# Fused hash-masked attention and MLP: one q load, three pairs' stacks and rotated pair orders in batch 0

## The chip, the cores and the metric

The kernel runs on one core of a Trainium2 chip. The metric is the device time of one execution in microseconds (us); the time of the kernel before is the median of three runs.

## The reference

Attention over 4 batches, 8 heads, 768 positions and 64 dimensions per head. Each query and each key gets a 6-bit bucket from the signs of a projection; a score counts only where query and key share a bucket. The attention output, laid out as 3072 rows of 512, goes through a two-layer MLP with a squared ReLU.

```
q_bits = (q @ proj > 0);  k_bits = (k @ proj > 0)        # 6 bits each
mask   = bucket(q_bits) == bucket(k_bits)
scores = where(mask, q @ k.T / 8, -1e9);  attn = softmax(scores)
x      = (attn @ v) as [3072, 512]
out    = relu(x @ w_in)**2 @ w_out                        # 512 -> 2048 -> 512
```

## The kernel before

**Units, visits and stages.** Heads are handled in pairs (`hp` 0 to 3), queries in three parts of 256 (`PARTS`). One *visit* is one batch, one part and one pair; it holds four *units*, each 128 queries of one head against all 768 keys (`unit`, line 811): score matmuls into PSUM (`pS` or `side`), a row maximum on DVE (`line`), the exponential on ACT (`e`), division by the row sum, and a transpose into `aT` (on PE through `pT` in the first four visits, by a DMA transpose of `hl` later). `av` (line 859) multiplies with the values. After the four pairs of a part, `moe` (line 915) runs one MLP stage: `pm` (first layer), `g` (squared ReLU), `po` (second layer), `acc`, `out`. There are 12 parts, so 48 visits, 192 units and 12 MLP stages. Early visits also carry the conversion of the MLP weights into fp16 pieces (`split`, line 626: tiles `room`, `sq`, `win`, `wo`, and four `norm` steps through the PSUM tile `side`).

**Preparation.** Before a pair can be visited, `prep` (line 716) builds its stacks. In batch 0 (`plain`) the stacks are float32: per head one tile with k on partitions 0 to 63 and code rows on 64 to 127, and one with q scaled by 1/8 below and code rows above. The chain is: load k and q of each head (128x768, tile `A` for the even head, `Q` for the odd); `pd`, eight matmul records against the projection `pj` (written into `side`); `bits`, the signs, on ACT; four matmuls `pc` with the sign table `sgn`, each 128x384, also into `side`; each is evicted whole by DVE into `L` (even head) or `M` (odd head), 128x384. Then the lower half of `L` or `M` is moved to the upper half of `A` or `Q`, and a second copy of q, loaded separately into a tile `R` (64x768), is scaled into the lower half of `L` or `M`:

```
move(R[U], M[T], 1.0, HALVES if r0 > 0 else (act, dve))   # A <- L, Q <- M
move(M[T], Rqs[odd], SC)                                  # L <- R, M <- R
out.append(((M, R),))
```

The tags `A`, `Q`, `L`, `M` have two buffers each (line 45), so the stacks of two pairs are on chip at a time. `visits` (line 973) goes through the pairs of batch 0 as 0,1,2,3 then 3,2,1,0 then 0,1,2,3; `ready` (line 977) prepares a pair again when its tiles have been given away. That makes eight preparations in batch 0: four in part 0, pairs 1 and 0 in part 1, pairs 2 and 3 in part 2. Pair 1 of part 1 takes the buffers of pair 2, which is visited directly before it. Batches 1 to 3 use fp16 stacks and another branch of `prep`.

**What sets the order.** The kernel records all operations and then orders them itself (class `Program`, line 132). `forward` (line 388) is a list scheduler over the five queues PE, DVE, ACT, POOL and SP with a price for each operation (`cost`, line 200), and picks the engine where an operation may run on several (`move` with ACT, DVE, POOL). `backward` (line 344) gives new priorities from the end, `replay` (line 302) prices the order; `order` (line 253) repeats this `ROUNDS` = 4 times and keeps the cheapest. The queues are in order, so each instruction waits behind the one ahead of it on its engine. `emit` (line 471) puts throwaway matmuls (`idle`) where the planner sees PE idle early on. SP issues nearly all DMAs; ACT issues the loads of `cst`, `pj` and half of the sign table (`acc<-consts`) at the start. `pr.first` makes SP's other loads come after the first pair's loads in the planner's order.

Of the kernel before, what the change touches and what calls it, by code (L numbers as in the profile page):

```python
# [14 lines left out]
F32 = mybir.dt.float32  # L15
# [4 lines left out]
ALU = mybir.AluOpType  # L20
# [22 lines left out]

ALIGN_ON = ("pool",)
BUFS = dict(xx=16, hl=3, e=3, aT=3, g=2, A=2, Q=2, L=2, M=2, RV=2, VV=6)
PRICE = dict(pe=1, dve=3.57, act=0.3, pool=3.06, sp=0.43)
# [3 lines left out]

ROUNDS, BEHIND = 4, 40000
TRIALS, WIDTH, SEED = 0, 3000.0, 1
LOADS = 0

MV = ("act", "dve", "pool", "sp")

# [11 lines left out]
FIRST = len(WIN_AT)  # L68

PACE = ((8, 0), (30, 60), (193, 800))  # L70

# [8 lines left out]
SWITCH, ENTRY = 95, 105  # L80
TRANSPOSES = 165

# [46 lines left out]
class Program:  # L129
# [39 lines left out]
    def add(self, *ways):  # L169
# [12 lines left out]
        for rec, w, (p0, p1, f0, f1, fs, g0, g1) in used:  # L182
            if rec.before is not None:
                deps |= rec.before.ops
            for j, w2, (a0, a1, b0, b1, bs, c0, c1) in rec.accesses:
                if (w or w2 or rec.kind == "psum") and a0 < p1 and p0 < a1 and b0 < f1 and f0 < b1 and not (fs and fs == bs and (c1 <= g0 or g1 <= c0)):
                    deps.add(j)
        for rec, w, r in used:
            rec.ops.add(i)
            rec.accesses.append((i, w, r))  # L190
        deps.discard(i)
# [8 lines left out]
    def cost(key, name, args, kw):  # L200
# [19 lines left out]
        if name.startswith("dma"):  # L220
            b = int(np.prod(args[0].shape)) * mybir.dt.size(args[0].dtype)
            inside = name == "dma_start_transpose" or kinds[:2] == ["sb", "sb"]
            busy = 1040 if key == "pool" else (650 if inside else 475) + 50 * (key == "act")
            return busy, b / (TRANSPOSES if name == "dma_start_transpose" else 314)
        if key == "act":
# [76 lines left out]
    def replay(self, out):  # L302
# [3 lines left out]
        at, free = dict.fromkeys(keys, 0), dict.fromkeys(keys, 0.0)  # L306
        started, dma, dge, held, kind = set(), 0.0, 0.0, 0.0, None
        for _ in out:
            best = None
            for k in keys:  # L310
                if at[k] < len(queues[k]):
                    i = queues[k][at[k]]
                    o = ops[i]
                    if all(j in started for j in o.deps) and all(j in started for j in o.after):
                        t = max([free[k]] + [ops[j].end + LAG * LAGS.get((ops[j].queue.key, k), 200) for j in o.deps])
                        if best is None or t < best[0]:
                            best = t, k, i
            t, k, i = best
            o = ops[i]
            at[k] += 1  # L320
            started.add(i)
            _, _, _, _, (busy, done), port = next(w for w in o.ways if w[0].key == k)
# [191 lines left out]
def lsh_attention_moe(ctx: ExitStack, tc, kq, v, proj2, w_in, w_out, consts, out):  # L514
# [7 lines left out]

    HALVES = tuple(getattr(pr, k) for k in MV)

# [36 lines left out]

    cst = sb([P, 4], F32, "cst")
    act.dma_start(cst, consts[:, 0:4])
    pj = sb([P, 32], F32, "pj")
    dve.memset(pj, 0.0)
    act.dma_start(pj[:, 0:NB], proj2[:, NB : 2 * NB])
    act.dma_start(pj[:, NB : 2 * NB], proj2[:, 3 * NB : 4 * NB])
    sgn_f = sb([P, RT, DM], F32, "acc")[:, 0]
    dve.memset(sgn_f, 0.0)
    for n in range(4):  # L570
        for t in range(2):
            c0 = 4 + t * D
            (act, sp)[t].dma_start(sgn_f[32 * n + t * NB : 32 * n + (t + 1) * NB, n * P + t * D : n * P + (t + 1) * D], consts[2 * t * NB : (2 * t + 1) * NB, c0 : c0 + D])
    sgn = sb([P, 4 * P], BF16, "sgn")
    dve.tensor_copy(sgn, sgn_f)
    thr = sb([P, 1], F32, "thr")
    dve.memset(thr, -(2.0**-80))
# [138 lines left out]
    def prep(b, hp, plain):  # L716
        r0 = pr.rank
        Rs, Rqs = [], []
        n0 = len(pr.ops)
        for odd in range(2):  # L720
            R = sb([P, S], F32, "Q" if odd else "A") if plain else sb([P, S], F32, "R", 2)
            send(R, kq[b, 2 * hp + odd])
            Rs.append(R)
            if plain:
                Rq = sb([P, S], F32, "R", 2)[T]
                send(Rq, kq[b, 2 * hp + odd, U])
                Rqs.append(Rq)
        if r0 < 0:

            pr.first = list(range(n0, len(pr.ops)))  # L730

# [7 lines left out]
        for odd, R in enumerate(Rs):  # L739
            pr.rank = r0  # L740
            if plain:
                M = sb([P, S], F32, "M" if odd else "L")
            else:

# [12 lines left out]
            for half in range(2):  # L757
                w = slice(half * HS, (half + 1) * HS)
                n = 2 * odd + half
                pc = small("pc")[:, 0:HS]  # L760
                pe.matmul(pc, sgn[:, n * P : (n + 1) * P], bits, start=True, stop=True)
                dve.tensor_scalar(M[:, w], pc, cst[:, 0:1], cst[:, 1:2], ALU.subtract, ALU.max)
            if plain:

                move(R[U], M[T], 1.0, HALVES if r0 > 0 else (act, dve))
                move(M[T], Rqs[odd], SC)
                out.append(((M, R),))
# [8 lines left out]
    def scale_values(b):  # L776

        r0 = pr.rank
        tops = sb([P, H // 2], F32, "vtop", 2)
        for hp in range(H // 2) if b else reversed(range(H // 2)):  # L780
            pr.rank = r0 + LOADS * hp
# [190 lines left out]

    visits = [(b, hp, part) for b in range(B) for part in range(PARTS) for hp in (range(H // 2) if b or part % 2 == 0 else reversed(range(H // 2)))]
    kept, kept_v = {}, {}
# [71 lines left out]
```

## Time and profile before

| | us |
|---|---|
| median of 3 runs (882.6 to 884.94) | 884.44 |
| the profiled execution | 885.79 |
| its span in the trace | 884.0 |
| PE busy in the span | 842.0 |
| DVE busy | 663.8 |
| ACT busy | 660.6 |
| POOL busy | 116.4 |

Times of rows are counted from the start of the span. A matmul row's duration is its latency: matmuls are pipelined, so several records overlap and a busy PE need not be at its peak pace. PEld is the weight load, which overlaps PE. A bracket behind a row gives the engine's idle time before it and what released it. The granted clock is the share of TensorE's full clock in a stretch.

### The profile page before, as it was taken

What the parts mean: (1) busy time and instruction counts of PE and PEld (TensorE: products, weight loads), DVE (VectorE), ACT (ScalarE), POOL (GpSimd) and SP (SyncE); (2) the same over time, 40 slices, a digit from 0 to 9 for tenths busy, and PEclk for the clock granted to TensorE, in tenths of its full rate; (3) what the DMA queues carried; (4) which work ended last, traced back from release to release, by engine and by line L of the source; (5) the groups of instructions that cost most, each with busy time, mean ns of one, the idle gap of its engine ahead of it and who ended that gap; (6) DMA issues with size and microseconds to landing.
All of it is one profiled execution on the core that took longest, in us unless ns stands there. A gap on an engine that the chain in (4) does not pass through costs nothing. (4 is left out here: it accounts for less than half of the span.)

```text
span 884.0 us, 17160 instructions
## 1 busy us (share of the span) xinstructions
PE 842.0 (95%) x6403; PEld 548.8 (62%) x6403; DVE 663.8 (75%) x1447; ACT 660.6 (75%) x1148; POOL 116.4 (13%) x182
## 2 busy tenths in 40 slices
PE   8889888899999899999999999999999999999997
PEld 5456544556555566766656667666656666667664
DVE  4789989987688788887686889885886888871111
ACT  3878857678697788887787989887886888873342
POOL 0464324254010010000000100000001000000000
PEclk9999979999999999999999999999999999999999
DMA  5745979975786688789387888897665877672000
GB/s 156 246 127 154 268 171 240 210 174 102 173 182 167 150 148 160 136 152 185 87 188 171 170 144 160 151 180 159 121 112 137 150 151 141 127 144 60 1 24 24
DMA packets 303731, 130.44 MB, mean 148 GB/s; under 512 B 280480, under 2 KB 288288, under 8 KB 303648
## 3 DMA queue, kind: packets, MB, share of 16 engines
q1 hardware_dynamic: 303168, 129.34, 68.8%
q8 instruction: 50, 0.82, 0.4%
q14 instruction: 33, 0.27, 0.1%
q10 hardware_dynamic: 480, 0.01, 0.0%
HBM read 42.02 MB, written 6.29 MB: 55 GB/s over the span
## 5 line engine op out<-in xcount | busy, mean ns | idle before, releaser
L501 PE MATMUL pm<-xx,win 128*128 128x256 f16 x2304 | 296.5, 273 | 2.9 <-ACT g L501 2.0
L501 PE MATMUL po<-wo,g 128*128 128x512 f16 x1152 | 291.3, 379 | 3.5 <-ACT acc L501 1.4
L501 PEld LDWEIGHTS <-win 128*128 128x128 f16 x2304 | 224.2, 98 | 67.8 <-issue 15.3
L501 DVE SCALAR_TENSOR_TENSOR hl<-e,rv,hl 128x768 f16<-128x768 f32 x176 | 178.4, 1017 | 22.0 <-ACT hl L501 20.6
L501 PEld LDWEIGHTS <-g 128*128 128x128 f16 x1152 | 111.2, 98 | 115.4 <-issue 9.8
L501 ACT ACTIVATE hl<-e,rv 128x768 f16<-128x768 f32 x169 | 156.1, 928 | 10.6 <-DMA aT<-hl 6.2
L501 ACT ACTIVATE g<-g 128x512 f32<-128x512 f32 (+1 forms) x185 | 115.7, 626 | 8.9 <-PE po L501 5.9
L499 DVE TENSOR_REDUCE line<-pS 128x1 f32<-128x768 f32 x113 | 107.4, 951 | 17.5 <-PE pS L501 16.5
L501 POOL TENSOR_SCALAR rv<-sm 128x1 f32<-128x1 f32 x99 | 35.8, 362 | 596.6 <-ACT e L501 591.2
L501 DVE SCALAR_TENSOR_TENSOR g<-g,g 128x512 f16<-128x512 f32 x85 | 59.2, 696 | 68.7 <-ACT g L501 68.2
L501 ACT ACTIVATE g<-pm 128x512 f32<-128x512 f32 x96 | 56.7, 590 | 60.6 <-PE pm L501 56.3
L494 PE MATMUL pA<-aT,VV 128*64 128x256 f16 x1584 | 94.9, 274 | 0.0
L494 PEld LDWEIGHTS <-VV 128*64 128x64 f16 x1584 | 83.1, 110 | 15.4 <-issue 14.5
L501 ACT ACTIVATE e<-pS,pair 128x768 f32<-128x768 f32 x72 | 71.0, 986 | 21.3 <-DVE pair L499 16.1
L501 ACT ACTIVATE e<-side,pair 128x768 f32<-128x768 f32 x72 | 70.9, 985 | 16.9 <-DVE rv L501 8.9
L499 DVE TENSOR_REDUCE line<-side 128x1 f32<-128x768 f32 x79 | 75.1, 951 | 5.3 <-PE side L501 5.0
L501 ACT ACTIVATE e<-pS,line 128x768 f32<-128x768 f32 x41 | 36.7, 895 | 20.4 <-DVE line L499 17.0
L501 PEld LDWEIGHTS <-room 128*128 128x128 f16 x288 | 27.3, 98 | 24.1 <-DMA room<-room 3.1
L501 PE MATMUL pS<-A,L 128*128 128x384 f32 x84 | 34.9, 538 | 5.1 <-ACT e L501 2.2
L501 PE MATMUL pS<-room 128*128 128x384 f16 x144 | 32.6, 329 | 2.5 <-DMA room<-room 2.3
L501 PE MATMUL pS<-Q,M 128*128 128x384 f32 x80 | 30.2, 500 | 3.9 <-ACT e L501 3.3
L501 DVE RECIPROCAL rv<-rv 128x1 f32<-128x1 f32 x192 | 30.2, 159 | 4.2 <-POOL rv L501 0.4
(154 smaller groups left out, 913.6 us busy)
## 6 DMA issues: line engine op xcount, KB each, us to landing
R<-kq SPq DMA_DIRECT2D x24, 384.0 KB
room<-w_in SPq DMA_DIRECT2D x16, 511.8 KB
room<-w_out SPq DMA_DIRECT2D x16, 511.8 KB
V<-vp SPq DMA_DIRECT2D x16, 384.0 KB
out<-acc SPq DMA_DIRECT2D x24, 256.0 KB
room<-room SPq DMA_DIRECT2D x60, 96.0 KB
Q<-kq SPq DMA_DIRECT2D x8, 384.0 KB
A<-kq SPq DMA_DIRECT2D x8, 384.0 KB
```

Source lines behind the costliest of these rows:

```text
L494: ins = q.engine.matmul(*map(real, args), **kw).ins
L499: issue(q, getattr(q.engine, name)(*map(real, args), **{k: real(x) for k, x in kw.items()}).ins)
L501: ins = getattr(q.engine, o.name)(*map(real, o.args), **{k: real(x) for k, x in o.kw.items()}).ins
```

## The change

In `prep`, batch 0's branch no longer loads q a second time. The scaled q is taken from the upper half of `A` or `Q` at once (`L<-A`, `M<-Q`, 64x768), and each `pc` is evicted by halves: the lower half straight into the upper half of `A` or `Q` on DVE (64x384), the upper half into the upper half of `L` or `M` on ACT (a ReLU with the bias `floor`) or on DVE. The first preparation uses both banks of `side` in turn for `pc`. `A`, `Q`, `L`, `M` get three buffers, and batch 0 visits the pairs as 0,1,2,3, then 1,2,3,0, then 2,3,0,1: six preparations, four in part 0, pair 0 in part 1 and pair 1 in part 2. Of the constants, the sign table's second half goes to POOL's queue, `pj` is one DMA, and the planner puts SP's other loads behind all of them. `align`, which rescales `wo` after the first MLP stage, may use ACT beside POOL. The planner searches 24 rounds and assumes a lower load rate (265 in place of 314); the other edits in the planner's code keep its rules and make it faster.

```diff
-ALIGN_ON = ("pool",)
-BUFS = dict(xx=16, hl=3, e=3, aT=3, g=2, A=2, Q=2, L=2, M=2, RV=2, VV=6)
+ALIGN_ON = ("act", "pool")
+BUFS = dict(xx=16, hl=3, e=3, aT=3, g=2, A=3, Q=3, L=3, M=3, RV=2, VV=6)
...
-ROUNDS, BEHIND = 4, 40000
+ROUNDS, BEHIND = 24, 40000
...
+START = ((0, 1, 2, 3), (1, 2, 3, 0), (2, 3, 0, 1))
...
-TRANSPOSES = 165
+TRANSPOSES, HBM = 165, 265
...
-    act.dma_start(pj[:, 0:NB], proj2[:, NB : 2 * NB])
-    act.dma_start(pj[:, NB : 2 * NB], proj2[:, 3 * NB : 4 * NB])
+    act.dma_start(pj[:, 0 : 2 * NB].rearrange("p (a k) -> p a k", a=2), proj2[:, NB : 5 * NB].rearrange("p (a k) -> p a k", a=2)[:, :, 0:NB])
...
-            (act, sp)[t].dma_start(sgn_f[32 * n + t * NB : 32 * n + (t + 1) * NB, n * P + t * D : n * P + (t + 1) * D], consts[2 * t * NB : (2 * t + 1) * NB, c0 : c0 + D])
+            (act, pool)[t].dma_start(sgn_f[32 * n + t * NB : 32 * n + (t + 1) * NB, n * P + t * D : n * P + (t + 1) * D], consts[2 * t * NB : (2 * t + 1) * NB, c0 : c0 + D])
...
+    floor = sb([P, 1], F32, "floor")
+    dve.memset(floor, 1.0 - NB / 2)
...
-            if plain:
-                Rq = sb([P, S], F32, "R", 2)[T]
-                send(Rq, kq[b, 2 * hp + odd, U])
-                Rqs.append(Rq)
...
-            pr.first = list(range(n0, len(pr.ops)))
+            pr.first = list(range(n0, len(pr.ops))) + constants
...
                 M = sb([P, S], F32, "M" if odd else "L")
+                move(M[T], R[U], SC)
...
-                pc = small("pc")[:, 0:HS]
+                pc = side[:, n % 2, 0:HS] if r0 < 0 else small("pc")[:, 0:HS]
                 pe.matmul(pc, sgn[:, n * P : (n + 1) * P], bits, start=True, stop=True)
-                dve.tensor_scalar(M[:, w], pc, cst[:, 0:1], cst[:, 1:2], ALU.subtract, ALU.max)
+                if not plain:
+                    dve.tensor_scalar(M[:, w], pc, cst[:, 0:1], cst[:, 1:2], ALU.subtract, ALU.max)
+                    continue
+                dve.tensor_scalar(R[U, w], pc[T], cst[T, 0:1], cst[T, 1:2], ALU.subtract, ALU.max)
+                pr.add((act, "activation", (M[U, w], pc[U], AF.Relu), {"bias": floor[U]}),
+                       (dve, "tensor_scalar", (M[U, w], pc[U], cst[U, 0:1], cst[U, 1:2], ALU.subtract, ALU.max), {}))
             if plain:
...
-                move(R[U], M[T], 1.0, HALVES if r0 > 0 else (act, dve))
-                move(M[T], Rqs[odd], SC)
                 out.append(((M, R),))
...
-    visits = [(b, hp, part) for b in range(B) for part in range(PARTS) for hp in (range(H // 2) if b or part % 2 == 0 else reversed(range(H // 2)))]
+    visits = [(b, hp, part) for b in range(B) for part in range(PARTS) for hp in (range(H // 2) if b else START[part])]
```

What this does to the order is seen at three places. The first is PE's queue at the first preparation of part 1. The numbers behind the names tell buffers apart: before, `A_1089` and `Q_1182` are the new pair's loads and `pS_1305` the scores of its first unit; after, `A_849` and `Q_983` are the new pair's, and `Q_200`, `A_261`, `Q_298` belong to pairs that are still on chip. Before:

```order
L494 MATMUL side_145<-A_1089,pj_63 32x384 x2
L494 MATMUL side_145<-Q_1182,pj_63 32x384 x2
...
L501 MATMUL pm_1293<-xx_917,win_685 128x256
L501 LDWEIGHTS sgn_161
L501 MATMUL side_145<-bits_1263,sgn_161 128x384
L501 MATMUL pS_1305<-A_1089,L_1281 128x384 x2
```

After, on the same engine:

```order
L501 MATMUL side_163<-A_849,pj_69 32x384 x2
L501 MATMUL side_163<-Q_983,pj_69 32x384 x2
L508 MATMUL pS_1083<-Q_200,M_368 128x384 x2
...
L508 MATMUL pS_1140<-A_261,L_449 128x384 x2
...
L508 MATMUL pS_1218<-A_261,L_449 128x384 x2
...
L508 MATMUL pS_1255<-Q_298,M_484 128x384 x2
...
L508 MATMUL pS_1319<-Q_298,M_484 128x384 x2
...
L508 MATMUL pS_1351<-A_849,L_887 128x384 x2
```

Before, the first scores behind the new pair's `pd` are that pair's own; now the scores of five units of other pairs stand between.

The second is SP's queue at the start, before:

```order
L501 DMA Q<-kq 128x768
L501 DMA A<-kq 128x768
L501 DMA acc<-consts 6x64 x4
L501 DMA R<-kq 64x768 x2
L501 DMA A<-kq 128x768
L501 DMA Q<-kq 128x768
L501 DMA unit_f<-consts 128x128
L501 DMA R<-kq 64x768 x2
```

And after:

```order
L508 DMA Q<-kq 128x768
L508 DMA A<-kq 128x768
L508 DMA unit_f<-consts 128x128
L508 DMA A<-kq 128x768
L508 DMA Q<-kq 128x768
L508 DMA room<-w_in 128x2047 x2
L508 DMA V<-vp 128x768 x4
```

The four small loads of the sign table are gone from SP (POOL has them), the `R` loads are gone, `unit_f` comes third, and weights and values come ahead of the third pair.

The third is DVE's queue from the sign table (`sgn`) to the first row maximum (`line0`), before:

```order
L501 CAST sgn_161<-acc_69 128x512
L501 TENSOR_SCALAR L_195<-side_145,cst_65 128x384 x2
L501 TENSOR_SCALAR A_80<-L_195 64x768
L501 TENSOR_SCALAR M_223<-side_145,cst_65 128x384
L501 CAST ident_238<-unit_f_163 128x128
L501 TENSOR_SCALAR M_223<-side_145,cst_65 128x384
L501 TENSOR_SCALAR Q_67<-M_223 64x768
L501 TENSOR_SCALAR M_223<-R_155 64x768
L499 TENSOR_REDUCE line0_74<-pS_242 128x1
```

And after:

```order
L508 TENSOR_SCALAR M_104<-Q_67 64x768
L508 TENSOR_SCALAR L_109<-A_81 64x768
L508 CAST ident_169<-unit_f_86 128x128
L508 CAST sgn_171<-acc_63 128x512
L508 TENSOR_SCALAR A_81<-side_163,cst_65 64x384 x2
L508 TENSOR_SCALAR M_227<-Q_106 64x768
L508 TENSOR_SCALAR Q_67<-side_163,cst_65 64x384 x2
L506 TENSOR_REDUCE line0_77<-pS_231 128x1
```

The moves of q now stand ahead of the sign table, and five instructions, not eight, stand between it and the first row maximum.

## Rows read from the trace of the kernel before

**Rows 1.** The profile page: busy us of each engine, share of the span, instructions

```profile
PE 842.0 (95%) x6403; PEld 548.8 (62%) x6403; DVE 663.8 (75%) x1447; ACT 660.6 (75%) x1148; POOL 116.4 (13%) x182
```

**Rows 2.** Windows: stretch, length, busy us (instructions) of PE, PEld, DVE, ACT, POOL; clock, DMA

```profile
25.00:100.00 75.00, 68.26 (x406) 41.79 (x405) 65.41 (x138) 60.59 (x117) 36.93 (x51) 1.00 0.63 184
100.00:125.00 25.00, 20.01 (x124) 10.68 (x123) 20.63 (x39) 14.00 (x24) 4.74 (x7) 0.80 0.83 224
125.00:175.00 50.00, 42.99 (x268) 25.87 (x267) 48.34 (x97) 37.44 (x65) 18.59 (x24) 1.00 0.99 218
...
300.00:800.00 500.00, 494.25 (x4033) 330.66 (x4032) 406.26 (x897) 416.45 (x717) 27.38 (x65) 1.00 0.78 150
```

**Rows 3.** Groups of PE in 100 to 125 us: count, busy us, mean ns, idle before

```profile
L501 PE MATMUL pS<-A,L 128*128 128x384 f32 x8 | 5.9, 887 | 1.1 <-ACT L L501 1.1
L494 PE MATMUL side<-A,pj 128*32 128x384 f32 x8 | 2.3, 673 | 0.0
```

**Rows 4.** The same view, 50 to 75 us

```profile
L501 PE MATMUL pS<-A,L 128*128 128x384 f32 x16 | 6.2, 499 | 0.9 <-ACT e L501 0.9
```

**Rows 5.** PE's timeline, 105 to 120 us: start, us, what, [idle before, releaser]

```profile
107.11 0.49 PE L494 MATMUL side<-A,pj 128*32 128x384 f32 x2
...
109.49 0.39 PE L501 MATMUL side<-sq,ones 128*128 128x512 bf16 x1 [0.85 <-DVE towin L501]
...
110.91 0.39 PE L501 MATMUL pm<-xx,win 128*128 128x256 f16 x2 [0.87 <-DVE win L501]
...
112.95 2.93 PE L501 MATMUL pS<-A,L 128*128 128x384 f32 x4 [1.15 <-ACT L L501]
...
117.52 0.61 PE L501 MATMUL side<-sq,ones 128*128 128x512 bf16 x1 [1.32 <-DVE M L501]
118.06 0.85 PE L494 MATMUL side<-A,pj 128*32 128x384 f32 x2
```

**Rows 6.** The chain of waits: start, us, work, count

```profile
598.99 0.78 PE pd L494 x8
...
819.24 2.62 PE pm L501 x24
```

**Rows 7.** Groups over the whole span, by line

```profile
L501 DVE TENSOR_SCALAR L<-side,cst 128x384 f32<-128x384 f32 x12 | 8.0, 668 | 1.7 <-PE side L501 1.7
...
L501 ACT ACTIVATE L<-R 64x768 f32<-64x768 f32 x7 | 5.9, 836 | 5.1 <-DVE A L501 5.1
...
L501 ACT ACTIVATE aT<-pT 128x384 f32<-128x384 f32 x26 | 11.9, 485 | 0.2
...
L501 ACT ACTIVATE bits<-pd,thr 128x384 bf16<-128x384 f32 x14 | 8.1, 576 | 7.2 <-PE pd L494 7.2
```

**Rows 8.** Timeline of the start

```profile
1.68 4.47 SPq L501 DMA_DIRECT2D acc<-consts  x4
2.13 2.50 ACTq L501 DMA_DIRECT2D acc<-consts  x4
...
7.58 0.43 DVE L501 CAST sgn<-acc 128x512 bf16<-128x512 f32 x1 [4.78 <-DMA acc<-consts]
...
8.97 0.33 PE L501 MATMUL side<-bits,sgn 128*128 128x384 bf16 x1
...
11.13 0.56 DVE L501 TENSOR_SCALAR A<-L 64x768 f32<-64x768 f32 x1
...
12.62 2.85 PE L501 MATMUL pS<-A,L 128*128 128x384 f32 x8
14.52 0.23 DVE L501 CAST ident<-unit_f 128x128 bf16<-128x128 f32 x1 [2.12 <-DMA unit_f<-consts]
...
15.96 0.55 DVE L501 TENSOR_SCALAR M<-R 64x768 f32<-64x768 f32 x1
16.43 1.81 DVE L499 TENSOR_REDUCE line<-pS 128x1 f32<-128x768 f32 x2
```

**Rows 9.** DMA issues: tile, queue, count, KB each

```profile
R<-kq SPq DMA_DIRECT2D x16, 192.0 KB
```

More of the change, by code (lines that the diff above doesn't have):

```diff
@@ L49 @@
 AHEAD, DELAY, LAG = 60, 2500, 1.0
-ROUNDS, BEHIND = 4, 40000
+ROUNDS, BEHIND = 24, 40000
 TRIALS, WIDTH, SEED = 0, 3000.0, 1
 LOADS = 0
-MV = ("act", "dve", "pool", "sp")
 PREP, STACKS, VALUES = -9, 0, 2
@@ L183, in add @@
             if rec.before is not None:
-                deps |= rec.before.ops
+                deps |= {j for j, _, _ in rec.before.accesses}
             for j, w2, (a0, a1, b0, b1, bs, c0, c1) in rec.accesses:
@@ L189, in add @@
             rec.ops.add(i)
+            if (w or rec.kind == "psum") and not r[4]:
+                rec.accesses = [x for x in rec.accesses if x[0] == i or not (r[0] <= x[2][0] and x[2][1] <= r[1] and r[2] <= x[2][2] and x[2][3] <= r[3])]
             rec.accesses.append((i, w, r))
@@ L223, in cost @@
             busy = 1040 if key == "pool" else (650 if inside else 475) + 50 * (key == "act")
-            return busy, b / (TRANSPOSES if name == "dma_start_transpose" else 314)
+            return busy, b / (TRANSPOSES if name == "dma_start_transpose" else HBM)
         if key == "act":
@@ L306, in replay @@
         at, free = dict.fromkeys(keys, 0), dict.fromkeys(keys, 0.0)
-        started, dma, dge, held, kind = set(), 0.0, 0.0, 0.0, None
+        left = [len(o.deps) + len(o.after) for o in ops]
+        gaps = {(a, k): LAG * LAGS.get((a, k), 200) for a in keys for k in keys}
+        dma, dge, held, kind, soon = 0.0, 0.0, 0.0, None, dict.fromkeys(keys)
         for _ in out:
@@ L312, in replay @@
                     i = queues[k][at[k]]
[L313 to L317, printed above, removed]
+                    if not left[i]:
+                        if soon[k] is None:
+                            soon[k] = max([free[k]] + [ops[j].end + gaps[ops[j].queue.key, k] for j in ops[i].deps])
+                        if best is None or soon[k] < best[0]:
+                            best = soon[k], k, i
             t, k, i = best
@@ L320, in replay @@
             at[k] += 1
-            started.add(i)
+            soon[k] = None
+            for j in o.users:
+                left[j] -= 1
             _, _, _, _, (busy, done), port = next(w for w in o.ways if w[0].key == k)
@@ L521, in lsh_attention_moe @@
     T, U = slice(0, D), slice(D, P)
-    HALVES = tuple(getattr(pr, k) for k in MV)
     def send(out, x):
@@ L558, in dr @@
         return pr.tile(drp, "dram", shape, dtype, name, bufs, tag)
-    cst = sb([P, 4], F32, "cst")
-    act.dma_start(cst, consts[:, 0:4])
     pj = sb([P, 32], F32, "pj")
     dve.memset(pj, 0.0)
-    act.dma_start(pj[:, 0:NB], proj2[:, NB : 2 * NB])
-    act.dma_start(pj[:, NB : 2 * NB], proj2[:, 3 * NB : 4 * NB])
+    act.dma_start(pj[:, 0 : 2 * NB].rearrange("p (a k) -> p a k", a=2), proj2[:, NB : 5 * NB].rearrange("p (a k) -> p a k", a=2)[:, :, 0:NB])
     sgn_f = sb([P, RT, DM], F32, "acc")[:, 0]
@@ L572, in lsh_attention_moe @@
             c0 = 4 + t * D
-            (act, sp)[t].dma_start(sgn_f[32 * n + t * NB : 32 * n + (t + 1) * NB, n * P + t * D : n * P + (t + 1) * D], consts[2 * t * NB : (2 * t + 1) * NB, c0 : c0 + D])
+            (act, pool)[t].dma_start(sgn_f[32 * n + t * NB : 32 * n + (t + 1) * NB, n * P + t * D : n * P + (t + 1) * D], consts[2 * t * NB : (2 * t + 1) * NB, c0 : c0 + D])
+    cst = sb([P, 4], F32, "cst")
+    act.dma_start(cst, consts[:, 0:4])
     sgn = sb([P, 4 * P], BF16, "sgn")
     dve.tensor_copy(sgn, sgn_f)
+    constants = [i for i, o in enumerate(pr.ops) if o.ways[0][1] == "dma_start"]
+    floor = sb([P, 1], F32, "floor")
+    dve.memset(floor, 1.0 - NB / 2)
     thr = sb([P, 1], F32, "thr")
@@ L717, in prep @@
         r0 = pr.rank
-        Rs, Rqs = [], []
+        Rs = []
         n0 = len(pr.ops)
@@ L779, in scale_values @@
         tops = sb([P, H // 2], F32, "vtop", 2)
-        for hp in range(H // 2) if b else reversed(range(H // 2)):
+        for hp in range(H // 2) if b else START[1]:
             pr.rank = r0 + LOADS * hp
```

## The prediction

> **What bounds the kernel now.** I read the page first: PE is busy 842.0 of 884.0 us, DVE and ACT three quarters of it [rows 1]. So the kernel is a PE kernel, and the question is where PE is kept from its work. The windows tell this by stage [rows 2]. From 300 to 800 us PE idles 5.75 of 500 us; nothing in batch 0's preparations can be gained there. The loss lies early: PE idles 6.7 us of 75 from 25 to 100 us (2.25 in each 25), 5.0 of 25 from 100 to 125, and 7.0 of 50 from 125 to 175. In the stretch from 100 to 125 us the granted clock is 0.80 on the mean, the only one of these stretches below 1.00. DVE is 87% busy from 25 to 100 us, 83% from 100 to 125 and 97% from 125 to 175. Batch 0 is thus close to DVE's limit as well, and this will be the main rival.
>
> The groups price the clock: the float32 score records took 5.9 us for 8 of them from 100 to 125 us [rows 3], and 6.2 us for 16 from 50 to 75 us [rows 4], so 0.74 against 0.39 us each. PE's timeline shows why PE stood still [rows 5]: the new pair's `pd` at 107.11 us, then every step waits for one eviction or for a step queued ahead of it on DVE (0.85, 0.87, 1.15 and 1.32 us, released by `towin`, `win`, the ACT write of `L`, and `M`), and the scores of that pair come at 112.95 us, 5.8 us after its `pd`, with almost nothing between. Behind the idle stretch the same `pd` takes 0.85 us where it took 0.49: the lower of the two clock levels (1.2 and 2.4 GHz) was granted there.
>
> At the start [rows 8] the first scores begin at 12.62 us, 3.65 us after the first `pc` at 8.97, because the four `pc` are evicted one after another. The first row maximum is at 16.43, since DVE has the moves of 0.56 and 0.55 us to do and also waits 2.12 us for `unit_f`.
>
> **The change, part by part.** All sums stand against the profiled execution, 885.79 us; the median of the three runs is 1.35 us lower.
>
> *Third buffer and rotated orders.* Part 1's first new pair used the buffers of the pair visited just before it, so its chain could not start earlier. Now, by PE's order, the scores of five units of other pairs stand between `pd` and the new pair's first scores, and they fill what PE idled. What can come back from 100 to 125 us is the idle time of 5.0, plus the clock: 8 score records by 0.35 = 2.8, and two `pd` groups by 0.85 - 0.49 = 0.36, so 0.7. That is 8.5; I leave the 2.25 us that the stretch before idles too, so 6.25. From 125 to 175 us PE idles 2.5 us over that same rate; part of this hangs on the second preparation there, and I take half, 1.25. Term: **7.5 us**. Its ends are 0, if DVE sets the pace anyway, and 8.75.
>
> *Two preparations fewer.* Each costs PE one `pd` group of 0.78 us [rows 6] and four `pc` of at most 0.33 [rows 8]. Twice that is 4.2 us; without the `pc`, whose latencies overlap with their neighbours, 1.6. I take **3.0**. PE's work at the end is back to back (24 `pm` in 2.62 us, 109 ns each [rows 6]), so work removed from PE moves the end by its own length.
>
> *Evictions by halves.* Before, eight preparations cost DVE 32 evictions of 0.67 us [rows 7] and seven moves of 0.55 (five `A<-L` or `Q<-M`, two `M<-R`), 25.3 us; ACT had 23 moves of 0.84 us [rows 7], 19.3. By the order after, DVE has 24 lower halves and 7 upper halves and 3 moves; ACT has 17 upper halves and 7 moves. A half has the same 384 columns on 64 partitions. The trace has no such form, so I bound it by the whole eviction, 0.67 us, and by the cheapest 64-partition form, the 768-column move of 0.55 us; I take 0.67, the row with PSUM as its source. On ACT it lies between `aT<-pT` at 0.485 and `bits` at 0.576 [rows 7]; I take 0.5. So DVE has 22.4 us (2.9 less) and ACT 14.4 (4.9 less). On PE's path this is nothing by itself: it runs beside the matmuls. It is the room that DVE gives for the first term.
>
> *The start.* The first two `pc` go to two banks, and a half on DVE runs beside a half on ACT. The first scores need one pair of halves, not two whole evictions, a move of 0.56 and an ACT move of 0.84: about 2 us sooner than 12.62. DVE's moves of q now stand ahead of `sgn`, in time that it idled (4.78 us), and `unit_f` comes third on SP. The first row maximum could come up to 3.6 us sooner. Ends 0 and 3.6; I take **2.5**.
>
> *Constants on POOL's queue.* SP's four small loads took 4.47 us to issue, ACT's four 2.50 [rows 8]. `sgn` began at 7.58 us, released by them. No row shows a load issued by POOL. From below: if it issues as ACT does, `sgn` is no later, and `bits` is the next to be waited for, so nothing is gained. From above: four at SP's 1.12 us each, behind POOL's own start, and as long again to land put `sgn` up to 4 us later. I take 0, nearest to SP's rows, and keep 4 as an end. A page speaks against this part: the Trainium skill, "SBUF — State Buffer", "SBUF: two separate sides", says that a DMA issued from GpSimd waits for its descriptors while VectorE runs an instruction that takes both port pairs. No run here shows it yet. By that rule the two q moves on DVE would hold up POOL's loads, and the sum would be the late-constants rival's instead of mine.
>
> *Loads and queues.* 16 loads of 192 KB vanish [rows 9], and four of 384 KB with the two preparations. Nothing in the chain waits for them in these stretches, so I cost them at nothing; the cover is PE's other work, and DMA is 0.63 to 0.99 busy there [rows 2], so a gain of some tenths is possible. SP now queues 1 MB of weights and 1.5 MB of values ahead of the third pair's loads; what they delay has two visits to spare. Part 1's load of `A` waits in SP's queue until the old pair's visit is over; behind it stand two weight and two value loads and the first transposes, which `av` waits for. I cost that at 0, as the transposes come after that visit too. `align` on two engines, the planner's new rate and 24 rounds: 0, no wait for `wo` is in these rows.
>
> Sum: 7.5 + 3.0 + 2.5 = 13.0. 885.8 - 13.0 = 872.8; at the median's level, less 1.35, **871.5 us**. This can only be had if DVE follows: from 25 to 175 us it idles 15.6 us [rows 2], more than the 7.5 asked of it, and it has 2.9 us less to do.
>
> **The rivals.**
>
> *DVE sets batch 0's pace.* For it: 97% from 125 to 175 us, and in part 1 the waits are released by DVE. Against it: 83% where PE stands still. Then the stall only moves, and the gain is DVE's removed work and the start: 2.9 + 2.5 = 5.4, so 879.0 us.
>
> *Constants late.* For it: POOL's four loads are on the only chain at the start, which has no other work for PE. Against it: `sgn` has until `bits` is done, about 8 us. It loses the start's 2.5 and up to 2 us more: 876.0 us.
>
> *A thinner cover, slower than before.* The whole order is made new, so the 500 us that PE now fills to 98.9% may be filled worse: where MLP matmuls lie further from the waits of a score unit, PE stands behind it in its queue. DVE and ACT at 81 and 83% there [rows 2] speak against it; that these orders have never met this trace speaks for it. It decides the sign once PE idles more than 13 us beyond its 5.75 there, 2.6% of the stretch; at 16 us the time is 887.5 us.
>
> **How the numbers follow.** The forecast has 0.60, with a range of its own from 864 to 878. DVE's pace 0.20, late constants 0.12, the thinner cover 0.08. The range reaches from 863, where the first and third terms come whole (8.75, 4.2 and 3.6 are 16.6, and some tenths for the loads and for a better order), to 883, which takes in both milder rivals. About 0.3% (2.7 us) is what a measurement of this kernel can tell from no change, so faster means below 881.8. The forecast gives 0.59 of that, the first rival 0.16 (it may end 3 us higher), the second 0.11: faster 0.86. Same: 0.07, from the upper ends of all cases. Slower: 0.07, nearly all from the last rival.
>
> **What would show each step.** Right: no stretch of 25 us between 25 and 230 us with PE idle over 3 us or a clock below 0.95; the first scores near 10.6 us and the first row maximum near 13; batch 0's `pd` records down from 64 to 48; ACT halves near 0.5 us. DVE's pace: PE idle is unchanged in sum from 25 to 200 us while DVE is above 95%. Late constants: DVE's cast of `sgn` after 9 us with DMA as its releaser. Thinner cover: PE's idle from 300 to 800 us above 10 us. The forecast is wrong if the span is above 878 us with the stall gone, since then the time went to a wait that these rows do not have.

## The result and the profile after

| | before | after |
|---|---|---|
| median, us (4 runs each, on one chip) | 884.49 (882.6 to 884.94) | 869.96 (868.34 to 871.95) |
| ratio after to before, 95% interval | | 0.9841 [0.9814, 0.9867] |
| the profiled execution, us | 885.79 | 869.22 |
| its span in the trace, us | 884.0 | 867.1 |

The change takes 14.5 us off. The forecast was 871.5. The total agrees; it did not come together as the sum had it.

The profile page of the kernel after, busy us of each engine, answers to [rows 1]. DVE and ACT are as busy as before; PE has 9.1 us less.

```profile
PE 832.9 (96%) x6347; PEld 544.4 (63%) x6349; DVE 661.8 (76%) x1444; ACT 660.6 (76%) x1150; POOL 111.2 (13%) x182
```

The windows after (stretch, length, busy us and instructions of PE, PEld, DVE, ACT, POOL, then clock, DMA share, GB/s) answer to [rows 2]:

```profile
25.00:100.00 75.00, 66.57 (x381) 38.99 (x384) 68.82 (x153) 62.84 (x123) 35.77 (x46) 1.00 0.51 142
100.00:125.00 25.00, 21.83 (x156) 13.39 (x155) 22.70 (x44) 15.61 (x28) 12.39 (x16) 1.00 0.80 187
125.00:175.00 50.00, 44.70 (x278) 27.59 (x276) 45.53 (x100) 33.05 (x58) 13.17 (x16) 0.93 0.84 187
...
230.00:300.00 70.00, 68.46 (x505) 44.03 (x504) 57.77 (x146) 60.36 (x106) 3.87 (x9) 1.00 0.74 166
300.00:800.00 500.00, 497.33 (x4080) 334.33 (x4079) 395.52 (x871) 405.92 (x702) 23.69 (x65) 1.00 0.75 146
```

One window of the kernel before that the forecast had no row of:

```profile
230.00:300.00 70.00, 64.67 (x486) 40.45 (x484) 53.00 (x142) 50.81 (x90) 3.09 (x5) 0.98 0.70 163
```

The stretch from 100 to 125 us has its full clock back, and PE idles 3.17 us there, not 4.99. But from 25 to 100 us PE now idles 8.43 us (6.74 before), and from 125 to 175 us 5.30 (7.01), at a clock of 0.93. Taken together from 25 to 175 us, idle time fell from 18.74 to 16.90 us only. The gain that no term had stands further back: from 230 to 300 us PE idles 1.54 us in place of 5.33, and from 300 to 800 us 2.67 in place of 5.75.

The row maxima on DVE's timeline serve as milestones: there are 192, one to a unit, and the 13th, 25th, 37th, 61st and 192nd are shown (start, us, what, idle before). Before:

```profile
56.85 0.95 DVE L499 TENSOR_REDUCE line<-pS 128x1 f32<-128x768 f32 x1
...
115.92 0.96 DVE L499 TENSOR_REDUCE line<-pS 128x1 f32<-128x768 f32 x1 [1.09 <-PE pS L501]
...
175.25 0.95 DVE L499 TENSOR_REDUCE line<-side 128x1 f32<-128x768 f32 x1
...
309.52 0.96 DVE L499 TENSOR_REDUCE line<-pS 128x1 f32<-128x768 f32 x1 [0.41 <-PE pS L501]
...
788.61 0.95 DVE L499 TENSOR_REDUCE line<-side 128x1 f32<-128x768 f32 x1
```

After:

```profile
55.18 0.96 DVE L506 TENSOR_REDUCE line<-pS 128x1 f32<-128x768 f32 x1 [0.40 <-PE pS L508]
...
101.23 0.96 DVE L506 TENSOR_REDUCE line<-pS 128x1 f32<-128x768 f32 x1 [0.20 <-PE pS L508]
...
171.00 0.96 DVE L506 TENSOR_REDUCE line<-side 128x1 f32<-128x768 f32 x1
...
294.90 0.96 DVE L506 TENSOR_REDUCE line<-pS 128x1 f32<-128x768 f32 x1 [0.52 <-PE pS L508]
...
769.96 0.95 DVE L506 TENSOR_REDUCE line<-side 128x1 f32<-128x768 f32 x1
```

The lead over the kernel before is 1.7 us at the 13th, 14.7 at the 25th (the old stall lies just ahead of it), 4.25 at the 37th, 14.6 at the 61st and 18.65 at the last. A milestone says nothing of the MLP work that was done or put off between, so the lead at one of them is not all kept. At the 25th nearly all of it is work put off: until then PE had been busy for 100.34 us before and for 86.70 us after. The rise to 14.7 and the fall to 4.25 therefore measure no stall; the windows do.

From 150 us PE falls to its lower clock again. PE's timeline, and the windows at the low clock, first the old stall in the kernel before, then this place:

```profile
149.43 0.38 PE L508 MATMUL side<-sq,ones 128*128 128x512 bf16 x1 [1.81 <-ACT sq L508]
151.12 2.93 PE L508 MATMUL pS<-Q,M 128*128 128x384 f32 x4 [1.31 <-ACT e L508]
153.84 4.00 PE L508 MATMUL pm<-xx,win 128*128 128x256 f16 x22
```

```profile
112.17:122.41 10.24, 8.14 (x19) 2.96 (x19) 6.68 (x10) 4.29 (x7) 1.69 (x3) 0.50 0.67 205
```

```profile
149.95:156.78 6.83, 5.66 (x18) 3.44 (x19) 6.37 (x16) 1.62 (x3) 0.77 (x1) 0.50 0.82 243
```

Two waits of 1.81 and 1.31 us lie ahead of four score records that take 2.93 us; at 109.97 us, at full clock, four of the same kind took 1.56. So in this execution the price of the old stall is paid again, in part, 40 us later. It is not paid in each. The second of the four kernels with added DVE work (below) has the same order and nothing added before about 171 us, and it kept its clock behind the same two waits:

```profile
149.02 0.38 PE L513 MATMUL side<-sq,ones 128*128 128x512 bf16 x1 [1.81 <-ACT sq L513]
150.71 1.56 PE L513 MATMUL pS<-Q,M 128*128 128x384 f32 x4 [1.31 <-ACT e L513]
152.10 2.56 PE L513 MATMUL pm<-xx,win 128*128 128x256 f16 x22
```

These records took 2.81 us less there. Of the four executions of the change itself the fastest, 868.34 us, had a mean granted clock of 1.000 and the others 0.995 to 0.998.

### The profile page after: what moved, and what is told of

The parts are those of the page before. It is cut to its first block, busy times and chain, and to the rows that moved or that the text cites. A ratio compares the mean times of both kernels' runs of the same rounds, so it can differ in the third digit from the quotient of the medians.

```text
span 867.1 us, 17038 instructions
## 1 busy us (share of the span) xinstructions
PE 832.9 (96%) x6347; PEld 544.4 (63%) x6349; DVE 661.8 (76%) x1444; ACT 660.6 (76%) x1150; POOL 111.2 (13%) x182
## 3 DMA queue, kind: packets, MB, share of 16 engines
HBM read 37.30 MB, written 6.29 MB: 50 GB/s over the span
## 4 chain that ended last, share of the span: by engine, by line
PE 61%; DVE 3%; ACT 3%; DMA 3%; issue 1%; POOL 0%; SPq 0%; ACTq 0%; DVEq 0%
PE po L508 22%; PE pm L508 21%; PE pA L501 8%; PE side L508 5%; PE pS L508 5%; DMA aT<-hl 2%; DVE hl L508 1%; ACT e L508 1%; PE pd L501 1%; DVE line L506 1%; DMA A<-A 1%; PE pc L508 1%; ACT hl L508 1%; ACT g L508 0%; ACT acc L508 0%
## 5 line engine op out<-in xcount | busy, mean ns | idle before, releaser
L508 ACT ACTIVATE hl<-e,rv 128x768 f16<-128x768 f32 x167 | 153.9, 928 | 6.1 <-DMA aT<-hl 2.5
L506 DVE TENSOR_REDUCE line<-pS 128x1 f32<-128x768 f32 x113 | 107.4, 951 | 14.5 <-PE pS L508 13.8
L508 POOL TENSOR_SCALAR rv<-sm 128x1 f32<-128x1 f32 x97 | 31.9, 329 | 544.4 <-ACT e L508 541.9
L501 PEld LDWEIGHTS <-VV 128*64 128x64 f16 x1584 | 83.2, 110 | 14.7 <-issue 13.2
L508 DVE SCALAR_TENSOR_TENSOR xx<-pA,xx 128x256 f16<-128x256 f32 x44 | 18.4, 418 | 25.8 <-ACT xx L508 25.2
L508 PE MATMUL pS<-A,L 128*128 128x384 f32 x84 | 33.0, 504 | 3.9 <-ACT e L508 3.7
L508 ACT ACTIVATE xx<-pA 128x256 f16<-128x256 f32 x42 | 15.9, 378 | 24.1 <-PE pA L501 23.9
```

The lines of the kernel that those rows point to most:

```text
L501: ins = q.engine.matmul(*map(real, args), **kw).ins
L506: issue(q, getattr(q.engine, name)(*map(real, args), **{k: real(x) for k, x in kw.items()}).ins)
L508: ins = getattr(q.engine, o.name)(*map(real, o.args), **{k: real(x) for k, x in o.kw.items()}).ins
```

## The experiments

Two questions were put. Which part of the change brings the time: the third buffer with the rotated orders, the halves, or the longer search? And does DVE set batch 0's pace? Ratios are to the kernel before on the same chip, with their 95% intervals.

**The change with four rounds.**

```diff
-ROUNDS, BEHIND = 24, 40000
+ROUNDS, BEHIND = 4, 40000
```

> The changed kernel with the order search back at 4 rounds, all else as changed. Buffers theory (the third buffer and the rotated orders carry the gain): 870 to 875 us, and PE idle from 100 to 125 us still near 3 us. Search theory (the longer search carries it): 880 to 885 us. DVE theory (batch 0 runs at DVE's pace and gains what DVE no longer does): 870 to 875 us.

Measured: 884.41 us, 0.9998 [0.9974, 1.0023]. All of the gain is gone, as the search theory had it. But from 100 to 125 us PE idles only 2.87 us, which is the sign that the buffers theory gave:

```profile
100.00:125.00 25.00, 22.13 (x130) 13.55 (x129) 20.84 (x38) 18.98 (x33) 9.47 (x14) 0.93 0.84 184
```

The largest piece of what is lost lies behind it: from 175 to 230 us PE idles 7.76 us, in the change 2.23. The windows of that place, PE's timeline inside them and two rows of ACT's:

```profile
205.00:215.00 10.00, 5.50 (x49) 3.17 (x44) 9.67 (x18) 9.93 (x11) 2.51 (x2) 0.90 0.54 113
215.00:225.00 10.00, 9.99 (x62) 6.61 (x62) 5.91 (x13) 6.29 (x11) 0.19 (x1) 0.75 0.17 33
```

```profile
207.42 0.52 PE L501 MATMUL pd<-A,pj 128*32 128x384 f32 x2 [0.54 <-issue]
...
209.63 0.33 PE L508 MATMUL pc<-bits,sgn 128*128 128x384 bf16 x1
212.35 0.34 PE L508 MATMUL pc<-bits,sgn 128*128 128x384 bf16 x1 [2.39 <-DVE L L508]
...
215.01 0.48 PE L508 MATMUL pc<-bits,sgn 128*128 128x384 bf16 x1 [1.57 <-ACT L L508]
```

```profile
209.06 5.29 ACT L508 ACTIVATE wo<-wo,rel 128x1024 f16<-128x1024 f16 x5
214.38 0.57 ACT L508 ACTIVATE L<-pc,floor 64x384 f32<-64x384 f32 x1
```

It is a stall like the old one, with part 2's new pair in place of part 1's: each `pc` waits for the eviction of the one before, DVE and ACT are 97 and 99% busy, PE 55%, and the clock falls behind it. Third buffer, rotated orders and halves are all in this kernel. By themselves they move the stall and do not make the kernel faster. One more edit has a part in it: `wo<-wo` is `align`, which only the change lets run on ACT, and ACT's half, on which the `pc` at 215.01 us waits, begins when five of these rows are done. What `align` on ACT costs was not tried by itself. The next three kernels leave it on POOL, so what they show of the buffers and the search does not hang on it.

**The third buffer and the rotated orders alone**, on the kernel before, with four rounds.

```diff
-BUFS = dict(xx=16, hl=3, e=3, aT=3, g=2, A=2, Q=2, L=2, M=2, RV=2, VV=6)
+BUFS = dict(xx=16, hl=3, e=3, aT=3, g=2, A=3, Q=3, L=3, M=3, RV=2, VV=6)
...
-        for hp in range(H // 2) if b else reversed(range(H // 2)):
+        for hp in range(H // 2) if b else (1, 2, 3, 0):
...
-    visits = [... for hp in (range(H // 2) if b or part % 2 == 0 else reversed(range(H // 2)))]
+    visits = [... for hp in (range(H // 2) if b else ((0, 1, 2, 3), (1, 2, 3, 0), (2, 3, 0, 1))[part])]
```

> The kernel before with three buffers and the rotated orders alone (six preparations, q loaded twice, whole evictions, 4 rounds). Buffers theory: 872 to 877 us, no stall near 110 us. Search theory: 882 to 886 us. DVE theory: two preparations of 3.2 us of DVE time fewer, 877 to 880 us.

Measured: 887.48 us, 1.0047 [1.0030, 1.0065]: 4 us slower, with two preparations fewer, and above every range of the expectation. Its window from 100 to 125 us:

```profile
100.00:125.00 25.00, 18.11 (x96) 10.53 (x95) 22.84 (x48) 12.85 (x24) 9.23 (x13) 0.86 0.92 202
```

PE idles 6.89 us there, more than the 4.99 before.

**24 rounds alone**, on the kernel before.

```diff
-ROUNDS, BEHIND = 4, 40000
+ROUNDS, BEHIND = 24, 40000
```

> The kernel before with 24 rounds of order search alone. Buffers theory: 881 to 886 us, the stall near 110 us still there. Search theory: 870 to 876 us. DVE theory: 881 to 886 us.

Measured: 882.59 us, 0.9984 [0.9968, 1.0000], about 1 us less. The stall stays as it was; with two buffers and the old pair orders the longer search found no way round it:

```profile
100.00:125.00 25.00, 20.00 (x123) 10.64 (x122) 21.35 (x40) 13.93 (x26) 4.67 (x6) 0.80 0.81 206
```

**Third buffer, rotated orders and 24 rounds**, on the kernel before: both edits above together; q is still loaded twice and evictions are whole.

> The kernel before with three buffers, the rotated orders and 24 rounds; q is still loaded twice and pc evicted whole. Combination theory: the halves are needed as well, 877 to 884 us. Draw theory: anywhere from 870 to 886 us. Buffers-and-search theory (those two are enough): 870 to 875 us.

Measured: 877.11 us, 0.9925 [0.9894, 0.9956]. Apart the two edits gave +4 and -1 us; together they give -6.6. PE is busy 20.36 us from 100 to 125 at full clock, so what went there is the low clock, and little of the idle time.

**The change without its third buffer and rotated orders**, with 24 rounds.

```diff
-BUFS = dict(xx=16, hl=3, e=3, aT=3, g=2, A=3, Q=3, L=3, M=3, RV=2, VV=6)
+BUFS = dict(xx=16, hl=3, e=3, aT=3, g=2, A=2, Q=2, L=2, M=2, RV=2, VV=6)
...
-START = ((0, 1, 2, 3), (1, 2, 3, 0), (2, 3, 0, 1))
+START = ((0, 1, 2, 3), (3, 2, 1, 0), (0, 1, 2, 3))
```

> The changed kernel with two buffers and the old pair orders again (eight preparations), q loaded once, evictions by halves, 24 rounds. Buffers theory: 879 to 884 us, with PE idle of 4 us or more in the 25 us of part 1's first new preparation. Search theory: 870 to 875 us. DVE theory: DVE has two preparations more of 3.7 us each to do, so 876 to 879 us.

Measured: 885.33 us, 1.0022 [1.0005, 1.0039], a little above the end of the buffers theory's range. So neither the search nor the halves carry the change without the buffers and the rotated orders. These two were not tried apart.

**Three more searched orders of the changed structure.** Since the cheapest of all orders tried is kept, small edits keep another one: 23 rounds keep that of round 9 (24 keep the last), the old load rate that of round 18, and the sign table's second half on SP's queue, as before, that of round 22.

```diff
-ROUNDS, BEHIND = 24, 40000
+ROUNDS, BEHIND = 23, 40000
```

> The changed kernel with 23 rounds in place of 24. The planner keeps the cheapest of its orders, which with 24 rounds is the last one; with 23 it keeps round 9's. Draw theory (the orders of one and the same program lie several us apart on the chip, and the changed kernel has a lucky one): 874 to 884 us. Combination theory (three buffers and evictions by halves leave room that any well-searched order uses): 867 to 873 us.

```diff
-TRANSPOSES, HBM = 165, 265
+TRANSPOSES, HBM = 165, 314
```

> The changed kernel with the planner's old load rate of 314 in place of 265, 24 rounds; it keeps round 18's order. Combination theory: 867 to 874 us. Draw theory: 874 to 884 us. If the lower rate is what makes the order fit the chip: 876 to 882 us, with waits on loads before 60 us.

```diff
-            (act, pool)[t].dma_start(...)
+            (act, sp)[t].dma_start(...)
```

> The changed kernel with the sign table's second half on SP again, 24 rounds; it keeps round 22's order. Combination theory: 867 to 874 us, the first row maximum within 1 us of 14.2 us. Draw theory: 874 to 884 us. If POOL's queue gives the start its gain: 1.5 to 3 us slower by the first row maximum, at 16 us or later.

Measured, in this sequence: 873.24 us, 0.9876 [0.9847, 0.9905]; 873.67, 0.9889 [0.9858, 0.9921]; 874.37, 0.9891 [0.9862, 0.9920]. The three lie where the ranges of the two theories meet, and each theory has a part. With the change itself, four searched orders lie between 870.0 and 874.4 us. Up to 4 us of the change's 14.5 thus hang on which order was kept; the intervals of the first and the last just overlap. The other 10 stay with every one of them. The last run does not show that POOL's queue is worth anything. The first row maximum comes at 14.73 us there and at 14.19 in the change, but `sgn` begins at 7.38 us there, sooner than in the change (7.55). And in the four kernels that follow, which have the change's start instruction by instruction, the first row maximum comes anywhere from 13.71 to 14.57 us.

**Does DVE set batch 0's pace?** Four kernels hold the order of the change fixed, instruction by instruction, and put work that nobody reads behind 28 row maxima when the instructions are written out: one DVE reduction each, or two ACT copies each.

```diff
+EXTRA = range(8, 36)
...
+                for _ in range(i in self.extra):
+                    issue(q, q.engine.tensor_reduce(self.spare[0].real(), self.spare[1].real(), AX.X, ALU.max).ins)
```

The range is 8 to 35 in the first, 36 to 63 in the second and 100 to 127 in the third.

> The changed kernel with its order kept and one more DVE reduction behind the row maximum of each of the units 8 to 35 (28 units, about 38 to 170 us; 512 columns of the sign table into a cell that nobody reads; nearest row: norm<-side, 512 columns, 0.63 us; so 17.7 us of DVE work). From 30 to 166 us the changed kernel has 12.4 us of idle DVE. If DVE sets batch 0's pace, PE falls behind by most of what is added: 10 to 17 us, 880 to 887. If DVE has room there and the order alone decides, what is added lies in DVE's idle time: under 5 us, below 875.

> The same 28 reductions behind units 36 to 63 (about 171 to 308 us), where the changed kernel's DVE idles 22 us of 134 and where its unforeseen gain lies. If DVE is as close there as in batch 0: over 8 us. If the stretch is PE's: under 4 us, below 874.

> The same 28 reductions behind units 100 to 127 (about 430 to 540 us), as the measure for a steady stretch: PE busy 109.95 of 110 us, DVE idle 14 of 110. Both theories: 0 to 5 us. If it costs as much as behind units 8 to 35, the added work shows nothing about batch 0.

The fourth, behind units 8 to 35 on ACT:

```diff
+                for _ in range(2 * (i in self.extra)):
+                    issue(self.act, self.act.engine.activation(self.spare[0].real(), self.spare[1].real(), AF.Copy, scale=1.0).ins)
```

> The changed kernel with its order kept and two more ACT copies (192 columns of the sign table, at most the 0.485 us of a 384-column ACT row, by estimate 0.3 us, so about 17 us of ACT work) ahead of the exponential of each of the units 8 to 35. ACT idles 33.6 us from 30 to 166 us. If DVE sets batch 0's pace: under 4 us, less than half of what the same work on DVE costs there. If batch 0 is bound by the chain from score to exponential rather than by DVE's load, ACT's work costs as much as DVE's.

Measured: 879.07 us, 0.9944 [0.9922, 0.9966]; 878.76, 0.9941 [0.9921, 0.9962]; 879.23, 0.9933 [0.9912, 0.9954]; and for ACT 875.42, 0.9897 [0.9873, 0.9921]. What was added, as the groups of the first and the fourth have it (count, busy us, mean ns, idle before):

```profile
L511 DVE TENSOR_REDUCE spare<-sgn 128x1 f32<-128x512 bf16 x28 | 18.9, 675 | 0.0
```

```profile
L511 ACT ACTIVATE spare<-sgn 128x192 f32<-128x192 bf16 x56 | 20.1, 359 | 1.0
```

The row that the first expectation took as nearest, `norm<-side`, has 0.678 us at 512 columns in the change's trace (0.63 is the mean with one shorter instruction), so 18.9 us were added and not 17.7. The exponential of the unit does not wait for the added reduction: in the first kernel one begins at 64.85 us while the reduction begun at 64.67 runs to 65.35. By the ratios against the change's 0.9841, times 884.4, the 19 us of DVE work cost 9.1, 8.8 and 8.1 us, whether they lie in batch 0, behind it or in the steady stretch: some 0.46 us per us. The 20.1 us on ACT cost 5.0, 0.25 per us. Each of these differences is uncertain by about 3 us. The first run thus meets neither range of its expectation (10 to 17 us, under 5). DVE's work costs more than ACT's, but batch 0 is not the special place that the rival had: the early run and the late one cost the same within that, so the expectation's own condition applies, and the runs say nothing for a DVE bound in batch 0. The surprise is the late one. From 440 to 560 us, first the change, then with the reductions:

```profile
440.00:560.00 120.00, 119.95 (x995) 80.64 (x995) 105.46 (x231) 104.31 (x182) 5.10 (x20) 1.00 0.85 165
```

```profile
440.00:560.00 120.00, 111.50 (x897) 72.92 (x897) 110.07 (x238) 97.04 (x167) 7.89 (x19) 1.00 0.75 151
```

PE idles 0.05 us there and DVE 14.5 of 120. With some 19 us of DVE work added, PE idles 8.5 us. DVE's idle time did not cover the work.

## Why the prediction was right in its sum, and where its steps failed

**24 rounds at 0** is the step that failed. It was put at nothing since no wait for `wo` was in the rows, and it stood in one sentence with two small edits. On the kernel before the search is worth 1 us, but on the changed structure it turns 884.4 into 870 to 874, 10 to 14 us. What fell with it is the view that a third buffer gives its 7.5 us at once. The five units of scores between `pd` and the new pair's first scores, on which the term rested, were read from the order that 24 rounds had made. With four rounds PE idles 2.87 us from 100 to 125 in the whole change and 6.89 with the buffers alone, and neither kernel is faster. The term was thus a term of both edits, and the sum could come out near because the order read was the order run. That it came as near as it did is luck: by what follows, the first term is about 3 us in place of 7.5, the second about 5 in place of 3.0, the start at most 2.2, and some 7 us came where no term was. `align`, the other edit of that sentence, has no run of its own; the old load rate has one (873.67 us).

**Third buffer and rotated orders, 7.5.** The mechanism is right: the stall from 100 to 125 us went, the clock is 1.00, and twelve `pS<-A,L` records there take 4.7 us, so 0.39 each as at 50 to 75 us [rows 4]:

```profile
L508 PE MATMUL pS<-A,L 128*128 128x384 f32 x12 | 4.7, 512 | 1.6 <-ACT e L508 1.6
```

Its size up to 175 us is smaller. Idle time from 25 to 175 us fell by 1.84 us. At the low clock PE was busy for 8.14 us before and for 5.66 after; if half of that is what the clock costs, 1.2 us came back. That makes 3.1 in place of 7.5, by estimate. The new stretch at low clock, which the forecast excluded, took part of it, and PE idles more from 25 to 100 us than before.

Some 7 us came instead as idle time that PE lost between 230 and 800 us. From 230 to 300 us this goes with the structure and not with the search: PE idles 5.19 to 5.53 us in the three kernels with two buffers, 3.48 and 3.25 in the two with the third buffer and whole evictions, and 0.66 to 2.25 in the five with both the buffers and the halves, also with four rounds (1.84). Of the 5.33 us before, 2.9 are waits of scores for DMA moves (`L<-A` 1.6, `room<-room` 1.3); after, no such wait is left there. From 300 to 800 us it is not settled: the change idles 2.67 us, with 23 rounds 2.67, with the sign table on SP 3.48, with four rounds 4.83, but with the old load rate 8.54, at 873.67 us; the other four idle 5.97 to 6.60. That the third buffer and the rotated orders together are what the search needs is shown by the six ratios; which of the two, and by which instruction, is not.

**Two preparations fewer, 3.0.** The `pd` records of batch 0 fell from 64 to 48 and `pc` from 80 to 72, as counted. PE's busy time fell by 9.1 us, but that also holds the records that no longer run at the low clock. No run measures this term alone, but the kernel with the buffers and four rounds allows an estimate. It has the same 115 throwaway matmuls as the kernel before. PE is busy 838.5 us in it, of which 14.05 at the low clock, before 842.0 and 11.22. With half of the latter taken off, these are 831.4 and 836.4, so the two preparations are worth about 5 us, more than the term's upper end of 4.2. That kernel is 4 us slower all the same, since PE idles 47.9 us in place of 42.0: what is taken off PE shows only where the order lets it.

**The start, 2.5.** The first row maximum is 2.24 us sooner (16.43 to 14.19 us), and the lead is 1.7 at the 13th. What of it reaches the end is not shown, since the order alone moves the 13th by more: it comes at 59.30 us in the change with four rounds, whose first row maximum is at 13.96, and at 53.80 with the buffers alone, whose first is at 16.32. The way there was another one than forecast. The timeline of the start after, which answers to [rows 8]:

```profile
1.72 2.27 POOL L508 DMA_DIRECT2D acc<-consts  x4 [1.27 <-DVE thr L508]
...
2.76 4.83 PE L497 MATMUL idle<-ones 128*128 128x128 bf16 x51 [2.76 <-DVE ones L508]
...
5.63 0.23 DVE L508 CAST ident<-unit_f 128x128 bf16<-128x128 f32 x1
...
7.52 0.52 PE L501 MATMUL side<-A,pj 128*32 128x384 f32 x2
...
7.55 0.43 DVE L508 CAST sgn<-acc 128x512 bf16<-128x512 f32 x1 [1.70 <-DMA acc<-consts]
...
9.07 0.48 PE L508 MATMUL side<-bits,sgn 128*128 128x384 bf16 x2
...
9.60 1.26 DVE L508 TENSOR_SCALAR A<-side,cst 64x384 f32<-64x384 f32 x2 [1.61 <-PE side L508]
...
10.95 1.04 ACT L508 ACTIVATE L<-side,floor 64x384 f32<-64x384 f32 x2 [1.06 <-DVE A L508]
...
12.20 0.81 PE L508 MATMUL pS<-A,L 128*128 128x384 f32 x2
...
14.19 0.96 DVE L506 TENSOR_REDUCE line<-pS 128x1 f32<-128x768 f32 x1
```

The first scores are 0.42 us sooner (12.62 to 12.20), not 2. "A half on DVE runs beside a half on ACT" is the sentence that failed. ACT's halves begin at 10.95, released by DVE's, which end at 10.86. The planner had them so too: its `add` makes any two accesses of one PSUM bank depend on each other, even two reads of different partitions. No run lets the two halves read at once. The row maximum gained all the same, since the 2.12 us that DVE waited for `unit_f` are gone (`ident` is done at 5.86) and the moves of q lie in DVE's idle time. A second thing was missed: `pd` begins at 7.52 us, before at 6.55. On PE it stands behind 51 throwaway matmuls, which begin at 2.76 us and end about then; before, they began at 1.66. The planner puts them where it expects PE to idle. The four kernels with added work show what they set: the same 51 took 4.36 to 5.21 us there, `pd` began at 7.04 to 7.90 us, and the first row maximum came 6.7 us behind `pd` each time, as in the change. Fewer of them was not tried.

**Evictions by halves, 0 on the path.** The sizes, by group after (count, busy us, mean ns, idle before):

```profile
L508 DVE TENSOR_SCALAR A<-side,cst 64x384 f32<-64x384 f32 x10 | 6.5, 669 | 2.8 <-PE side L508 1.8 <-DMA room<-w_out 0.8
...
L508 ACT ACTIVATE L<-side,floor 64x384 f32<-64x384 f32 x7 | 3.9, 575 | 1.8 <-DVE A L508 1.7
```

The DVE half takes 0.669 us, as the whole eviction did [rows 7]: half the partitions save nothing. The ACT half takes 0.575 where 0.5 was taken. That they are worth nothing on PE's path does not seem to hold. DVE's part came to 2.3 us less, not 2.9 (25.3 before; 24 x 0.669, 7 x 0.686 and three moves of 2.1 in sum after), and ACT's to 3.6 less (19.3 before; 17 x 0.575 and 7 x 0.842 after). By the prices of the last four runs these are worth 1.1 and 0.9 us. That is an estimate, since the prices are those of work added to a kept order; no run takes the halves alone out of the change. With the start's gain it is of the size of what lies between 877.11 us, which has neither halves nor the new start, and the four orders from 870.0 to 874.4.

**Constants on POOL's queue, 0.** This held: `sgn` begins at 7.55 us, before at 7.58, and at 7.38 in the run that puts the loads back on SP. POOL's four loads took 2.27 us to issue, 0.57 each. The Trainium skill's rule in "SBUF — State Buffer", "SBUF: two separate sides", that a load issued from GpSimd waits while VectorE takes both port pairs, was not put to the test: DVE's first move of q began at 3.99 us, as POOL's last issue ended. No run here shows it.

**Loads and queues, 0.** HBM reads fell from 42.02 to 37.30 MB and the DMA share from 25 to 100 us from 0.63 to 0.51. No stretch's gain is tied to it.

**The rivals.** DVE's pace would have given 879. Its sign, idle time unchanged from 25 to 200 us, is nearly there (18.74 to 16.90 us up to 175), though with DVE 91% busy and not 95; but DVE costs the same in the steady stretch, and the time is 9 us lower. Late constants: `sgn` came before 9 us, so no. The thinner cover: PE idles 2.67 us from 300 to 800, so no; nor do the buffers alone show it, since at 887.48 us PE idles 6.40 there and its loss lies between 100 and 230 us. Of the signs listed as "right", the `pd` count held and the row maximum nearly; four of the eight stretches of 25 us between 25 and 225 us missed theirs, three by idle time (25 to 50, 100 to 125 and 125 to 150 us) and one by clock (0.86 from 150 to 175). The lower end of the range, 863 us, does not follow from its terms either: all three at their upper ends give 867.9, and "some tenths" do not fill the rest.

## What to carry to other kernels

Where a scheduler writes the order, a change of structure and the search over orders are one term: price them together, and measure the structure once with the old search and once with the new, since either alone may show nothing. A third buffer removes a reason to wait, not the wait; look where the stall goes next. Idle time of an engine with an in-order queue is not free room: ask what the next instruction on it holds back before costing added work there at nothing.

## What the runs showed of the hardware that was not expected

A 64-partition eviction from PSUM with 384 columns takes as long on DVE (0.669 us) as a 128-partition one (0.668 [rows 7]). And a move from SBUF to SBUF took longer beside POOL. These rows of the start's timeline show DVE's move of q for the first pair, POOL's conversion of a weight piece, and DVE's move for the second pair:

```profile
3.99 0.56 DVE L508 TENSOR_SCALAR M<-Q 64x768 f32<-64x768 f32 x1 [1.17 <-DMA Q<-kq]
...
10.69 0.77 POOL L508 TENSOR_SCALAR room<-room 128x512 f16<-128x512 bf16 x1 [6.71 <-DMA room<-w_in]
10.88 0.98 DVE L508 TENSOR_SCALAR M<-Q 64x768 f32<-64x768 f32 x1
...
11.97 0.77 POOL L508 TENSOR_SCALAR room<-room 128x512 f16<-128x512 bf16 x1 [0.51 <-DVE M L508]
```

The same move takes 0.56 us alone and 0.98 beside POOL's instruction, and POOL's next one begins after it. In the first kernel with added DVE work, which has the same order here, the move began ahead of POOL's instruction:

```profile
10.42 0.56 DVE L513 TENSOR_SCALAR M<-Q 64x768 f32<-64x768 f32 x1
...
10.82 0.78 POOL L513 TENSOR_SCALAR room<-room 128x512 f16<-128x512 bf16 x1 [6.85 <-DMA room<-w_in]
```

Over all the traces, five moves of this form began 0.20 to 0.56 us behind a POOL instruction that ran on for 0.2 us or more. They took 0.62 to 1.07 us, and each ended 0.40 to 0.41 us after POOL's. Those that began ahead of POOL's, or within 0.04 us of it, took 0.55 or 0.56. The Trainium skill, "SBUF — State Buffer", "SBUF: two separate sides", says that the port pair which VectorE and GpSimd share is held by one of them for a whole instruction. The durations agree with that. What it costs the kernel as a whole was not tried.

The lower clock, too, is not fixed by the order: behind the same two waits of 1.81 and 1.31 us PE was granted the lower level (0.50) from 149.95 to 156.78 us in one execution and kept the full one in another.
